# A reordered first slot in a gated scan followed by a leaky two-layer MLP

## The chip, the core and the metric

The kernel runs on one core of one Trainium2 chip. The metric is the device time of one execution in microseconds (us). All inputs and outputs are fp32 in device memory.

## What is computed

There are 4 sequences of 6080 tokens of width 256, taken as one list of 24,320 tokens. First a gated scan along each sequence, then an MLP of width 2048 on every token:

```python
sig = 1.0 / (1.0 + np.exp(-f_logit))
f = lower_bound[None, None, :] + (1.0 - lower_bound[None, None, :]) * sig
for t in range(S):
    h = f[:, t] * h + (1.0 - f[:, t]) * x[:, t]
    y[:, t] = h
...
h = y @ w_in
g = np.maximum(0.01 * h, h)
out = g @ w_out
```

## The kernel before

**Precision.** A product of two fp32 matrices is made of three matmuls in a rounded fp32 type: each operand is split into a high part (ScalarE copies it with rounding) and a low part (VectorE subtracts the high part from the operand), and low x high, high x high and high x low are added up in PSUM. For the weights, `scale_w` (L91, two ScalarE instructions), `decode_w` (L101, two of VectorE and one of GpSimd) and `split_w` (L115, one of ScalarE and one of VectorE) take the raw 64-bit words apart and split them, group by group. `wi_h` and `wi_l` are the parts of w_in, `wo` holds those of w_out, `yh` and `yl` those of the scanned y, and `gh` and `gl` those of the activation.

**Blocks, groups, slots.** The tokens go through in 24 blocks of 1024 (the last has 768), each as two halves of 512. The width of 2048 is cut into 8 groups of 256. One (block, group) pair is a slot; there are 192, numbered s. A slot's first products are a 2 x 2 scheme over (half of the group h, token half t) and its second products multiply the activations by w_out. Block 0 uses `plain_slot` (L329): four quarters of 6 matmuls, and 24 second ones, 48 in all. The later blocks use `slot` (L356): seven products M1 to M7 of 3 matmuls on combined operands, and 24 second ones, 45 in all. Of the 24 second matmuls of a slot, those of quarter (0,0) run at the slot's own end and the other 18 in the next slot (`old`).

**Order.** Every engine runs its instructions in the order in which the program writes them, so the order in the source is the schedule. A slot calls `hook(name)` at fixed places (C, a0, A, a2, B, a3, D, E), and a table (L231) and the loop at L511 hang other work there:

```python
(2, "a0"): [("th", 0)],
(2, "A"): [("f", 0), ("tx", 0), ("tx", 1)],
```

In group 2 of each block the next block's x is thus turned by two VectorE transposes (`tx`, L201), straight after the gate `f`. In block 0 the hooks also prepare the weights of the next groups: scale and decode of w_out at C, its split at a2, scale and decode of the next w_in at B, its split at E. From slot 6 to slot 13 `combine_w` (five VectorE sums) and `split_c` make the combined weights of one group per slot, at D and E in block 0, at C and a3 in block 1.

**The first slot** (`first_slot`, L444) turns the first block with TensorE against an identity matrix (`turn_first`, 4 transposes for 512 tokens of one half of the width), runs `tanh` on ScalarE, the gate's multiply-add, the product `u` and the scan on VectorE, and splits w_in group 0 whole:

```python
tanh_first(0, 0)
scale_w("i", 0)
scan_first(0, 0)
decode_w("i", 0)
```

It then does the two quarters of token half 0 (L461, L463), turns and scans token half 1, does its two quarters, and the second products of quarter (0,0) (L488). The first 512 tokens are loaded in pieces of 256 KB, the second in pieces of 512 KB, all from SP's queue (L498 to L506); `lower_bound` comes from ScalarE's queue.

**Queues and buffers.** All other loads and all stores are issued by SP. `xld`, `lld` and the output tile `osb` share two buffers in turn. PSUM has two banks for `a`, one each for `b` and `c`, and four for the second products, which the first slot also uses for turning. `a` and `r`, the two tiles of a weight being decoded, have one buffer each. `gh` and `gl` have four each.

**The end.** After the last slot (L549) the open second products run, VectorE turns the four outputs into `osb` (L288), and SP issues eight stores (L293).

Of the kernel before, what the change touches and what calls it, by code (L numbers as in the profile page):

```python
# [24 lines left out]
def tile_gated_scan_then_leaky_mlp(  # L25
# [65 lines left out]
    def scale_w(kind, g):  # L91
        a = dw_p.tile([P, 2, 256], F32, tag="a", name="a")
        r = dw_p.tile([P, 2, 256], U32, tag="r", name="r")

        hi, lo = raw_t[kind, g][:, :, :, 1], raw_t[kind, g][:, :, :, 0]
        act(out=a, in_=hi.bitcast(F32), func=ACTF.Abs, scale=2.0 ** -112)

        act(out=r, in_=lo, func=ACTF.Copy, scale=2.0 ** -29)
        part_t[kind, g] = a, r

    def decode_w(kind, g):  # L101
        hi = raw_t.pop((kind, g))[:, :, :, 1]
        a, r = part_t[kind, g]
        w = dw_p.tile([P, 4, P], F32, tag="w", name="w", bufs=2)
        au = a.bitcast(U32)
# [5 lines left out]
        wu = w.rearrange("p (h k) f -> p h (k f)", h=2).bitcast(U32)  # L111
        nc.gpsimd.tensor_tensor(out=wu, in0=au, in1=r, op=ALU.add)
        part_t[kind, g] = w

    def split_w(kind, g):  # L115
        w = part_t.pop((kind, g))
# [65 lines left out]
    def form(j, i):  # L182
# [4 lines left out]
        if i == (0, 2):  # L187
            v = b[:, :, 0]
# [6 lines left out]
    def x_piece(j, piece):  # L195
# [38 lines left out]
        (2, "A"): [("f", 0), ("tx", 0), ("tx", 1)],  # L234
# [14 lines left out]
    def product(bank, j, g, m, start, stop=True):  # L249
# [3 lines left out]
        for s, (a, b) in enumerate(((wi_l, yh), (wi_h, yh), (wi_h, yl))):  # L253
            nc.tensor.matmul(  # L254
                out=bank[:, :n], lhsT=a[:, g, w, :], rhs=b[:, i, :n],
                start=start and s == 0, stop=stop and s == 2, skip_group_check=True,
# [6 lines left out]
    def second(j, g, h, t):  # L263
# [8 lines left out]
        for k, w, v, s in ((0, 1, gh, 0), (0, 0, gh, 1), (1, 1, gh, 0), (1, 0, gh, 1), (0, 0, gl, 2), (1, 0, gl, 2)):  # L272
# [312 lines left out]
```

## Time and profile before

| | us |
|---|---|
| median of 3 runs | 2036.8 |
| lowest and highest run | 2036.34, 2039.99 |
| the profiled execution | 2041.47 |
| its span, first to last instruction | 2039.7 |

The span is what the rows below are measured in: their times count from its start. The profiled execution is 4.67 us above the median. Engines are PE (TensorE; PEld are its weight loads), DVE (VectorE), ACT (ScalarE), POOL (GpSimd) and SP. An instruction's row has its start, its duration, engine, line, operation, output<-inputs and shape, and in brackets how long its engine stood idle before it and what ended that. Where a row says x2 or more, it stands for so many like instructions and the duration is from the start of the first to the end of the last. Matmul durations overlap: the distance from one start to the next is the price, not the duration. The granted clock PEclk is a share of 2.4 GHz. A row of the windows view has the stretch, its length, the busy time of PE, PEld, DVE, ACT and POOL in it (with instructions), the granted clock, the DMA engines' mean busy share and the GB/s.

### The profile page before, as it was taken

What the parts mean: (1) busy time and instruction counts of PE and PEld (TensorE: products, weight loads), DVE (VectorE), ACT (ScalarE), POOL (GpSimd) and SP (SyncE); (2) the same over time, 40 slices, a digit from 0 to 9 for tenths busy, and PEclk for the clock granted to TensorE, in tenths of its full rate; (3) what the DMA queues carried; (4) which work ended last, traced back from release to release, by engine and by line L of the source; (5) the groups of instructions that cost most, each with busy time, mean ns of one, the idle gap of its engine ahead of it and who ended that gap; (6) DMA issues with size and microseconds to landing.
All of it is one profiled execution on the core that took longest, in us unless ns stands there. A gap on an engine that the chain in (4) does not pass through costs nothing.

```text
span 2039.7 us, 23146 instructions
## 1 busy us (share of the span) xinstructions
PE 1991.5 (98%) x8696; PEld 1625.8 (80%) x8696; DVE 1419.9 (70%) x2003; ACT 1398.6 (69%) x2344; POOL 26.8 (1%) x24
## 2 busy tenths in 40 slices
PE   5899999999999999999999999999999999999998
PEld 4777787888878788888888788888888888888888
DVE  5887666766766767667676667676766777676664
ACT  4766666677666766777667666777666766776665
POOL 1200000000000000000000000000000000000000
PEclk8999999999999999999999999999999999999999
DMA  7351505326053141560613505325054051450211
GB/s 162 91 61 18 63 1 62 40 23 63 4 59 52 11 62 16 48 62 1 63 29 34 63 1 63 43 20 63 9 54 58 5 62 23 41 57 0 37 21 16
DMA packets 583392, 84.60 MB, mean 41 GB/s; under 512 B 574064, under 2 KB 581232, under 8 KB 583280
## 3 DMA queue, kind: packets, MB, share of 16 engines
q1 hardware_dynamic: 583008, 83.13, 33.6%
q8 instruction: 68, 1.11, 0.2%
q14 instruction: 44, 0.36, 0.1%
q10 hardware_dynamic: 272, 0.00, 0.0%
HBM read 58.20 MB, written 24.90 MB: 41 GB/s over the span
## 4 chain that ended last, share of the span: by engine, by line
PE 74%; DVE 8%; DMA 7%; ACT 5%; SPq 4%; issue 2%; POOL 0%; DVEq 0%; POOLq 0%
PE o L273 39%; PE pa L254 20%; PE pc L254 10%; DMA xld<-in_x_dram 7%; PE pb L254 5%; SPq L150 4%; DVE lT L201 2%; ACT c L305 2%; ACT gh L300 2%; DVE xT L201 1%; DVE gl L310 1%; DVE c L379 1%; DVE c L397 1%; ACT c L366 0%; DVE xT L174 0%
## 5 line engine op out<-in xcount | busy, mean ns | idle before, releaser
L273 PE MATMUL o<-gh,wo 128*128 128x512 f32 (+1 forms) x3072 | 821.1, 389 | 2.6 <-DVE wo L123 2.6
L310 DVE TENSOR_TENSOR gl<-c,gh 128x512 fp32r<-128x512 f32 (+1 forms) x768 | 526.5, 689 | 275.0 <-ACT c L305 275.0
L273 PEld LDWEIGHTS o<-gh,wo 128*128 128x128 f32 x3072 | 575.8, 188 | 124.0 <-issue 3.0
L300 ACT ACTIVATE gh<-c 128x512 fp32r<-128x512 f32 (+1 forms) x552 | 342.3, 620 | 198.2 <-DVE c L397 155.8
L273 PE MATMUL o<-gl,wo 128*128 128x512 f32 (+1 forms) x1536 | 473.8, 390 | 0.0
L305 ACT ACTIVATE c<-c 128x512 f32<-128x512 f32 (+1 forms) x552 | 346.5, 628 | 17.5
L273 PEld LDWEIGHTS o<-gl,wo 128*128 128x128 f32 x1536 | 288.3, 188 | 60.5
L254 PE MATMUL pa<-yh,wi_l 128*128 128x512 f32 (+1 forms) x768 | 302.8, 394 | 15.5 <-ACT yh L225 6.9
L254 PE MATMUL pa<-yl,wi_h 128*128 128x512 f32 (+1 forms) x768 | 300.5, 391 | 0.0
L254 PE MATMUL pa<-yh,wi_h 128*128 128x512 f32 (+1 forms) x768 | 299.7, 390 | 0.0
L378 ACT ACTIVATE c<-pa 128x512 f32<-128x512 f32 (+1 forms) x184 | 109.3, 594 | 184.9 <-PE pa L254 181.9
L373 ACT ACTIVATE c<-pa 128x512 f32<-128x512 f32 (+1 forms) x184 | 109.4, 594 | 172.8 <-PE pa L254 170.4
L379 DVE TENSOR_TENSOR c<-pc,c 128x512 f32<-128x512 f32 (+1 forms) x184 | 125.2, 681 | 98.2 <-ACT c L378 94.0
L254 PEld LDWEIGHTS pa<-yh,wi_l 128*128 128x128 f32 x768 | 144.9, 189 | 58.4 <-ACT c L366 12.7
L370 DVE TENSOR_TENSOR c<-pb,c 128x512 f32<-128x512 f32 (+1 forms) x184 | 125.8, 684 | 77.9 <-PE pb L254 66.0
L397 DVE TENSOR_TENSOR c<-pc,c 128x512 f32<-128x512 f32 (+1 forms) x184 | 125.9, 684 | 64.9 <-PE pc L254 64.3
L254 PEld LDWEIGHTS pa<-yl,wi_h 128*128 128x128 f32 x768 | 144.8, 189 | 30.9 <-DVE yl L228 1.0
L254 PEld LDWEIGHTS pa<-yh,wi_h 128*128 128x128 f32 x768 | 144.8, 189 | 30.0
L254 PE MATMUL pc<-yh,wi_l 128*128 128x512 f32 (+1 forms) x384 | 152.4, 397 | 9.9 <-DVE c L379 5.9
L254 PE MATMUL pc<-yl,wi_h 128*128 128x512 f32 (+1 forms) x384 | 150.0, 391 | 0.0
L254 PE MATMUL pc<-yh,wi_h 128*128 128x512 f32 (+1 forms) x384 | 149.7, 390 | 0.0
L300 ACT ACTIVATE gh<-pa 128x512 fp32r<-128x512 f32 (+1 forms) x200 | 115.8, 579 | 14.6 <-PE pa L254 14.6
(74 smaller groups left out, 1661.9 us busy)
## 6 DMA issues: line engine op xcount, KB each, us to landing
out_dram<-osb SPq DMA_DIRECT2D x184, 128.0 KB, 3.3
lld<-in_f_logit_dram SPq DMA_DIRECT2D x90, 256.0 KB, 6.6
xld<-in_x_dram SPq DMA_DIRECT2D x90, 256.0 KB, 5.8
raw<-in_moe_w_in_dram SPq DMA_DIRECT2D x16, 256.0 KB, 3.5
raw<-in_moe_w_out_dram SPq DMA_DIRECT2D x8, 512.0 KB, 3.7
lld<-in_f_logit_dram SPq DMA_DIRECT2D x4, 192.0 KB, 5.9
xld<-in_x_dram SPq DMA_DIRECT2D x4, 192.0 KB, 4.7
out_dram<-osb SPq DMA_DIRECT2D x8, 96.0 KB, 2.5
```

The source lines that it names most:

```text
L150: nc.sync.dma_start(out=t[32 * q:32 * q + 32], in_=v[q])
L201: nc.vector.transpose(out=xs[j, nm][:, k], in_=loaded[j, nm][:, k].rearrange("p t d -> p (t d)"))
L254: nc.tensor.matmul(out=bank[:, :n], lhsT=a[:, g, w, :], rhs=b[:, i, :n], start=start and s == 0, stop=stop and s == 2, skip_group_check=True,)
L273: nc.tensor.matmul(out=o[k][:, :n], lhsT=wo[:, g, h, w, k * P:(k + 1) * P], rhs=v[:, :n], start=first and s == 0, stop=last and s == 2, sk ...
L300: act(out=gh[:, :n], in_=src[:, :n], func=ACTF.Prelu, alpha=0.01)
L305: act(out=dst[:, :n], in_=src[:, :n], func=ACTF.Prelu, alpha=0.01)
L310: vtt(out=gl[:, :n], in0=c[:, :n], in1=gh[:, :n].bitcast(F32), op=ALU.subtract)
L370: vtt(out=c11[:, :n], in0=b[:, :n], in1=c11[:, :n], op=ALU.add)
L373: act(out=c12[:, :n], in_=a[:, :n], func=ACTF.Copy)
L378: act(out=c22[:, :n], in_=a[:, :n], func=ACTF.Copy)
L379: vtt(out=c22[:, :n], in0=c[:, :n], in1=c22[:, :n], op=ALU.add)
L397: vtt(out=c12[:, :n], in0=c[:, :n], in1=c12[:, :n], op=ALU.add)
```

## The change

The first slot's work is put in another order. w_in group 0 is scaled, decoded and split in two halves (`hs`); the two quarters of token half 0 are each opened with the operand half k=0, token half 1 is turned and scanned between their parts, and their k=1 parts follow. The gate's multiply-add goes to ScalarE. Short runs of matmuls of the identity with itself (`keep_busy`, result unused) are put before and between the turns. w_in group 1 is split within the first slot, and the second products of quarter (0,0) of slot 0 move into slot 1. In the plain slots the hooks move: w_out's split and w_in's scale and decode to a new W, ahead of `low` of the first quarter; w_in's split to a new V, ahead of the last leaky pair. In block 1 `combine_w` goes to B and `split_c` to E, at the slot's end. The x transposes move from A to B and a3. For the last block's closing second products the matmuls are sorted by output, and three of its eight stores are issued by ScalarE. The first piece of x is loaded from ScalarE's queue, ahead of `lower_bound`; the second 512 tokens come in 256 KB pieces; w_in 1 is loaded ahead of w_out 0.

The body of `first_slot` after the change (after the line `j, g = 0, 0`):

```python
        h0, h1 = slice(0, 1), slice(1, 2)
        keep_busy(5)
        turn_first(0, 0)
        keep_busy(2)
        turn_first(1, 0)
        keep_busy(4)
        gate_first(0, 0)
        u_first(0, 0)
        scale_w("i", 0, h0)
        decode_w("i", 0, h0)
        scan_first(0, 0)
        scale_w("i", 0, h1)
        decode_w("i", 0, h1)
        gate_first(1, 0)
        u_first(1, 0)
        high(0)
        split_w("i", 0, "hl", h0)
        lower(0)
        split_w("i", 0, "h", h1)
        p11 = plain_bank(0, 0)
        plain_halves(p11, j, g, 0, 0, 0, (1, 0, 2))
        turn_first(0, 1)
        gate_first(0, 1)
        scan_first(1, 0)
        split_w("i", 0, "l", h1)
        p21 = plain_bank(1, 0)
        plain_halves(p21, j, g, 1, 0, 0, (1, 2, 0))
        turn_first(1, 1)
        high(1)
        lower(1)
        gate_first(1, 1)
        u_first(0, 1)
        scan_first(0, 1)
        plain_halves(p11, j, g, 0, 0, 1)
        plain_halves(p21, j, g, 1, 0, 1)
        u_first(1, 1)
        scale_w("i", 1)
        high(3)
        scan_first(1, 1)
        decode_w("i", 1)
        lower(3)
        p22, p12 = plain_bank(1, 1), plain_bank(0, 1)
        plain_halves(p22, j, g, 1, 1, 0)
        plain_halves(p12, j, g, 0, 1, 0)
        high(2)
        lower(2)
        plain_halves(p22, j, g, 1, 1, 1)
        plain_halves(p12, j, g, 0, 1, 1)
        load_w("i", 2)
        load(1, "l")
        load_w("o", 1)
        load(1, "x")
        c11 = plain_leaky(j, g, 0, 0, p11)
        scale_w("o", 0)
        decode_w("o", 0)
        low((j, g, 0, 0), c11)
        split_w("i", 1, "hl")
        c22 = plain_leaky(j, g, 1, 1, p22)
        low((j, g, 1, 1), c22)
        split_w("o", 0, "hl")
        c21 = plain_leaky(j, g, 1, 0, p21)
        low((j, g, 1, 0), c21)
        c12 = plain_leaky(j, g, 0, 1, p12)
        low((j, g, 0, 1), c12)
```

The rest of the diff, its helpers of one line left out:

```diff
+    def scale_w(kind, g, hs=slice(0, 2)):
+        if (kind, g) not in part_t:
+            a = dw_p.tile([P, 2, 256], F32, tag="a", name="a")
+            r = dw_p.tile([P, 2, 256], U32, tag="r", name="r")
+            w = dw_p.tile([P, 4, P], F32, tag="w", name="w", bufs=2)
+            part_t[kind, g] = a, r, w
+        a, r, _ = part_t[kind, g]
+
+        hi, lo = raw_t[kind, g][:, hs, :, 1], raw_t[kind, g][:, hs, :, 0]
+        act(out=a[:, hs], in_=hi.bitcast(F32), func=ACTF.Abs, scale=2.0 ** -112)
+
+        act(out=r[:, hs], in_=lo, func=ACTF.Copy, scale=2.0 ** -29)
...
+        wu = w.rearrange("p (h k) f -> p h (k f)", h=2)[:, hs].bitcast(U32)
+        nc.gpsimd.tensor_tensor(out=wu, in0=au, in1=r[:, hs], op=ALU.add)
+
+    def split_w(kind, g, part, hs=slice(0, 2)):
+        w = part_t[kind, g][2].rearrange("p (h c) f -> p h c f", h=2)[:, hs]
         if kind == "i":
-            wh, wl = wi_h[:, g, 0:4], wi_l[:, g, 0:4]
+            wh, wl = (t[:, g, 0:4].rearrange("p (h c) f -> p h c f", h=2)[:, hs] for t in (wi_h, wi_l))
         else:
-            wh, wl = (wo[:, g, :, i, :].rearrange("p h (c f) -> p h c f", c=2) for i in range(2))
-            w = w.rearrange("p (h c) f -> p h c f", h=2)
-        act(out=wh, in_=w, func=ACTF.Copy)
-        vtt(out=wl, in0=w, in1=wh.bitcast(F32), op=ALU.subtract)
+            wh, wl = (wo[:, g, hs, i, :].rearrange("p h (c f) -> p h c f", c=2) for i in range(2))
+        if "h" in part:
+            act(out=wh, in_=w, func=ACTF.Copy)
+        if "l" in part:
+            vtt(out=wl, in0=w, in1=wh.bitcast(F32), op=ALU.subtract)
...
-        (2, "A"): [("f", 0), ("tx", 0), ("tx", 1)],
+        (2, "A"): [("f", 0)],
+        (2, "B"): [("tx", 0)],
+        (2, "a3"): [("tx", 1)],
...
-        for k, w, v, s in ((0, 1, gh, 0), (0, 0, gh, 1), (1, 1, gh, 0), (1, 0, gh, 1), (0, 0, gl, 2), (1, 0, gl, 2)):
+        order = ((0, 1, gh, 0), (0, 0, gh, 1), (1, 1, gh, 0), (1, 0, gh, 1), (0, 0, gl, 2), (1, 0, gl, 2))
+        if last and j == NB - 1:
+            order = sorted(order, key=lambda v: v[0])
+        for k, w, v, s in order:
...
-            nc.sync.dma_start(out=v[q][:, :, t * nb:(t + 1) * nb], in_=osb[32 * q:32 * q + 32])
+            e = nc.scalar if j == NB - 1 and (t or q > 1) and q % 2 else nc.sync
+            e.dma_start(out=v[q][:, :, t * nb:(t + 1) * nb], in_=osb[32 * q:32 * q + 32])
...
+    def plain_halves(bank, j, g, h, t, k, order=(0, 1, 2)):
+        product(bank, j, g, (2 * h + k, ((0, 1), (3, 2))[t][k]), k == 0, k == 1, order)
+
+    def plain_leaky(j, g, h, t, bank):
         c = new_c()
         leaky_high((j, g, h, t), bank)
         leaky((j, g, h, t), c, bank)
         return c
 
+    def plain_bank(h, t):
+        pool, tag = (ps_b, "bc"[h == 0]) if t else (ps_a, "a")
+        return pool.tile([P, HM], F32, tag=tag, name="p" + tag)
...
-        c11 = plain_quad(j, g, 0, 0, a)
+        c11 = plain_leaky(j, g, 0, 0, plain_quad(j, g, 0, 0))
+        if s == 1:
+            b = plain_quad(j, g, 1, 1)
+            second(j, 0, 0, 0)
         hook("a0")
         hook("A")
+        hook("W")
         old(s, 1, 1)
         low((j, g, 0, 0), c11)
-        b = ps_b.tile([P, HM], F32, tag="b", name="pb")
-        c22 = plain_quad(j, g, 1, 1, b)
-        hook("a2")
+        if s > 1:
+            b = plain_quad(j, g, 1, 1)
+        c22 = plain_leaky(j, g, 1, 1, b)
         hook("B")
         old(s, 1, 0)
         low((j, g, 1, 1), c22)
-        a = ps_a.tile([P, HM], F32, tag="a", name="pa")
-        c21 = plain_quad(j, g, 1, 0, a)
+        c21 = plain_leaky(j, g, 1, 0, plain_quad(j, g, 1, 0))
         hook("a3")
         hook("D")
         old(s, 0, 1)
         low((j, g, 1, 0), c21)
-        c = ps_b.tile([P, HM], F32, tag="c", name="pc")
-        c12 = plain_quad(j, g, 0, 1, c)
-        hook("E")
+        b = plain_quad(j, g, 0, 1)
+        hook("V")
+        c12 = plain_leaky(j, g, 0, 1, b)
         second(j, g, 0, 0)
         low((j, g, 0, 1), c12)
+        hook("E")
...
+    def turn_first(k, t):
+        for nm in "lx":
+            if t == 0:
+                pool, tag = (ps_b, "bc"["lx".index(nm)]) if k else (ps_a, "a")
+            else:
+                pool, tag = ps_o, f"o{k}{'lx'.index(nm)}"
+            o = pool.tile([P, 4, P], F32, tag=tag, name="p" + tag)
+            for u in range(4):
+                nc.tensor.transpose(o[:, u], loaded[0, nm][:, 4 * t + u, k * P:(k + 1) * P], ident)
+            parts[nm, k, t] = o.rearrange("p u n -> p (u n)")
+
+    def keep_busy(n):
+
+        o = ps_o.tile([P, HM], F32, tag="o11", name="po11")
+        for _ in range(n):
+            nc.tensor.matmul(out=o[:, :P], lhsT=ident, rhs=ident, start=True, stop=True)
+
+    def gate_first(k, t):
+        f = xs[0, "l"][:, k, t * HM:(t + 1) * HM]
+        act(out=f, in_=parts["l", k, t], func=ACTF.Tanh, scale=0.5)
+        act(out=f, in_=f, func=ACTF.Identity, scale=cc[:, k:k + 1], bias=cd[:, k:k + 1])
...
+        load_first(nc.sync, "l", 0, 0)
+        load_first(nc.scalar, "x", 0, 0)
+        nc.scalar.dma_start(out=lb, in_=lower_bound.rearrange("(k p) -> p k", p=P))
+        load_w("i", 0)
+        for k, t in ((1, 0), (0, 1), (1, 1)):
             for nm in "lx":
-                load_first(nm, 0, slice(k, k + 1))
-            if k == 0:
-                load_w("i", 0)
-        for nm in "lx":
-            load_first(nm, 1, slice(0, KC))
+                load_first(nc.sync, nm, t, k)
+        load_w("i", 1)
...
-                    elif at == "a2":
-                        split_w("o", g)
-                    elif at == "B" and g + 1 < NG:
-                        scale_w("i", g + 1)
-                        decode_w("i", g + 1)
-                        if g + 2 < NG:
-                            load_w("i", g + 2)
-                    elif at == "E" and g + 1 < NG:
-                        split_w("i", g + 1)
+                    elif at == "W":
+                        split_w("o", g, "hl")
+                        if g + 1 < NG:
+                            scale_w("i", g + 1)
+                            decode_w("i", g + 1)
+                            if g + 2 < NG:
+                                load_w("i", g + 2)
+                    elif at == "V" and g + 1 < NG:
+                        split_w("i", g + 1, "hl")
                 if j > 0 and (g, at) == (0, "C"):
                     new_osb(j - 1)
                     if j + 1 < NB:
                         load(j + 1, "l")
                 c = s + 2 - NG
                 if 0 <= c < NG:
-                    if at == ("D" if j == 0 else "C"):
+                    if at == ("D" if j == 0 else "B"):
                         combine_w(c)
-                    elif at == ("E" if j == 0 else "a3"):
+                    elif at == "E":
                         split_c(c)
                 if j > 0:
                     for p in hooks_own.get((g, at), ()):
```

## Rows read from the trace of the kernel before

**Rows 1.** The page, part 1: busy time, share, instructions.

```profile
PE 1991.5 (98%) x8696; PEld 1625.8 (80%) x8696; DVE 1419.9 (70%) x2003; ACT 1398.6 (69%) x2344; POOL 26.8 (1%) x24
```

**Rows 2.** PE's waits, 0 to 140 us: total, times, longest.

```profile
PE pa L254 <- ACT yh L225: 6.9, 1, 6.9
PE pa L254 <- DVE wi_l L123: 6.6, 6, 1.4
PE pb L254 <- ACT yh L225: 6.5, 1, 6.5
PE o L273 <- DVE wo L123: 2.6, 1, 2.6
```

**Rows 3.** The timeline of PE at five slot starts.

```profile
52.77 0.50 PE L254 MATMUL pa<-yh,wi_l 128*128 128x512 f32 x1 [1.04 <-DVE wi_l L123]
...
125.84 0.39 PE L254 MATMUL pa<-yh,wi_l 128*128 128x512 f32 x1
...
205.82 0.39 PE L254 MATMUL pa<-yh,wi_l 128*128 128x512 f32 x1
...
216.12 0.39 PE L254 MATMUL pa<-yh,wi_l 128*128 128x512 f32 x1
...
1964.89 0.33 PE L254 MATMUL pa<-yh,wi_l 128*128 128x384 f32 x1
```

**Rows 4.** A stretch by windows, and two products of the timeline after it.

```profile
30.00:32.00 2.00, 2.00 (x5) 1.50 (x6) 1.97 (x4) 0.00 (x0) 0.16 (x1) 0.50 0.91 80
...
33.00 0.63 PE L254 MATMUL pc<-yh,wi_h 128*128 128x512 f32 x1
...
33.42 0.63 PE L254 MATMUL pc<-yl,wi_h 128*128 128x512 f32 x1
```

**Rows 5.** The timeline of the first slot, four instructions.

```profile
4.40 1.09 PE L427 MATMUL pa<-ident,lld 128*128 128x128 f32 x4 [4.40 <-DMA lld<-in_f_logit_dram]
...
5.53 0.60 ACT L431 ACTIVATE lT<-pa 128x512 f32<-128x512 f32 x1 [2.99 <-PE pa L427]
...
7.63 1.22 DVE L174 TENSOR_TENSOR_SCAN xT<-lT,xT 128x512 f32<-128x512 f32 x1
...
9.21 0.69 DVE L107 SCALAR_TENSOR_TENSOR a<-a,raw 128x512 uint32<-128x512 uint32 x1
```

**Rows 6.** The timeline: GpSimd's add, a scan beside it, the gate.

```profile
66.87 2.12 POOL L112 TENSOR_TENSOR w<-a,r 128x512 uint32<-128x512 uint32 x1 [4.06 <-DVE a L107]
...
67.87 2.21 DVE L174 TENSOR_TENSOR_SCAN xT<-lT,cy,xT 128x512 f32<-128x512 f32 x1
...
68.84 1.25 ACT L207 ACTIVATE lT<-lT,cd,cc 128x1024 f32<-128x1024 f32 x1
```

**Rows 7.** Windows: the fullest plain slot.

```profile
102.03:114.74 12.71, 11.28 (x49) 8.94 (x49) 10.92 (x20) 9.46 (x18) 3.18 (x2) 1.00 0.76 62
```

**Rows 8.** The timeline of a slot that turns x, and M6 behind.

```profile
320.75 0.39 PE L254 MATMUL pa<-yh,wi_l 128*128 128x512 f32 x1
...
326.90 0.63 ACT L305 ACTIVATE c<-c 128x512 f32<-128x512 f32 x1
...
327.17 2.37 DVE L201 STREAM_TRANSPOSE xT<-xld 128x1024 f32<-128x1024 f32 x2 [3.41 <-DMA xld<-in_x_dram]
...
332.09 0.68 DVE L397 TENSOR_TENSOR c<-pc,c 128x512 f32<-128x512 f32 x1
...
334.64 0.19 PEld L254 LDWEIGHTS pa<-yh,wi_l 128*128 128x128 f32 x1 [0.48 <-ACT c L366]
```

**Rows 9.** The end: SP's issues, their landing, two windows (of loads first).

```profile
2031.47 5.50 SPq L293 DMA_DIRECT2D out_dram<-osb  x8
...
out_dram<-osb SPq DMA_DIRECT2D x8, 96.0 KB, 2.5
...
28.00:30.00 2.00, 0.15 (x1) 0.16 (x1) 1.46 (x4) 1.15 (x2) 0.00 (x0) 0.50 1.60 145
2034.00:2035.00 1.00, 0.00 (x0) 0.00 (x0) 0.00 (x0) 0.00 (x0) 0.00 (x0) 0.73 0.92 138
```

More of the change, by code (lines that the diff above doesn't have):

```diff
@@ L89, in load_w, with decode_w @@
         raw_t[kind, g] = r
[L91 to L105, printed above, removed]
+    def scale_w(kind, g, hs=slice(0, 2)):
[8 more added lines that the diff above has]
+        act(out=r[:, hs], in_=lo, func=ACTF.Copy, scale=2.0 ** -29)
+    def decode_w(kind, g, hs=slice(0, 2)):
+        hi = raw_t[kind, g][:, hs, :, 1]
+        a, r, w = part_t[kind, g]
+        au = a[:, hs].bitcast(U32)
         nc.vector.tensor_scalar(out=hi, in0=hi, scalar1=0x80000000, scalar2=None, op0=ALU.bitwise_and)
@@ L246, in tile_gated_scan_then_leaky_mlp, with product @@
     hooks_own = {(0, "C"): [("l", (5, 7))]}
-    def product(bank, j, g, m, start, stop=True):
+    def product(bank, j, g, m, start, stop=True, order=(0, 1, 2)):
         yh, yl = ysplit[j]
@@ L252, in product @@
         w, i = m
-        for s, (a, b) in enumerate(((wi_l, yh), (wi_h, yh), (wi_h, yl))):
+        for e, s in enumerate(order):
+            a, b = ((wi_l, yh), (wi_h, yh), (wi_h, yl))[s]
             nc.tensor.matmul(
                 out=bank[:, :n], lhsT=a[:, g, w, :], rhs=b[:, i, :n],
-                start=start and s == 0, stop=stop and s == 2, skip_group_check=True,
+                start=start and e == 0, stop=stop and e == 2, skip_group_check=True,
             )
@@ L418, in load_first, with u_first @@
         )
[L420 to L433 removed]
+    def turn_first(k, t):
[16 more added lines that the diff above has]
+        act(out=f, in_=f, func=ACTF.Identity, scale=cc[:, k:k + 1], bias=cd[:, k:k + 1])
+    def u_first(k, t):
         r = slice(t * HM, (t + 1) * HM)
         f, u = xs[0, "l"][:, k, r], xs[0, "x"][:, k, r]
[L436 to L438 removed]
         nc.vector.scalar_tensor_tensor(
@@ L441, in scan_first, with high, lower @@
         )
-        scan(0, k, r.start, r.stop)
+    def scan_first(k, t):
+        scan(0, k, t * HM, (t + 1) * HM)
+    def high(i):
+        x_piece(0, ("h", (i, i + 1)))
+    def lower(i):
+        x_piece(0, ("l", (i, i + 1)))
     def first_slot():
         j, g = 0, 0
-        for nm, k in (("l", 0), ("x", 0), ("l", 1), ("x", 1)):
-            turn_first(nm, k, 0)
-        tanh_first(0, 0)
-        scale_w("i", 0)
-        scan_first(0, 0)
-        decode_w("i", 0)
-        tanh_first(1, 0)
@@ L454, in first_slot @@
-        split_w("i", 0)
-        scan_first(1, 0)
-        new_split(0)
-        x_piece(0, ("h", (0, 2)))
-        x_piece(0, ("l", (0, 2)))
-        scale_w("o", 0)
-        a = ps_a.tile([P, HM], F32, tag="a", name="pa")
-        c11 = plain_quad(j, g, 0, 0, a)
-        a = ps_a.tile([P, HM], F32, tag="a", name="pa")
-        c21 = plain_quad(j, g, 1, 0, a)
-        for nm, k in (("l", 0), ("x", 0), ("l", 1), ("x", 1)):
-            turn_first(nm, k, 1)
-        tanh_first(0, 1)
-        tanh_first(1, 1)
@@ L477, in first_slot @@
         load(1, "x")
-        scale_w("i", 1)
+        c11 = plain_leaky(j, g, 0, 0, p11)
+        scale_w("o", 0)
+        decode_w("o", 0)
         low((j, g, 0, 0), c11)
-        low((j, g, 1, 0), c21)
-        b = ps_b.tile([P, HM], F32, tag="b", name="pb")
-        c22 = plain_quad(j, g, 1, 1, b)
-        decode_w("i", 1)
-        split_w("o", 0)
-        c = ps_b.tile([P, HM], F32, tag="c", name="pc")
-        c12 = plain_quad(j, g, 0, 1, c)
-        low((j, g, 1, 1), c22)
-        second(j, g, 0, 0)
-        split_w("i", 1)
+        split_w("i", 1, "hl")
+        c22 = plain_leaky(j, g, 1, 1, p22)
+        low((j, g, 1, 1), c22)
+        split_w("o", 0, "hl")
+        c21 = plain_leaky(j, g, 1, 0, p21)
+        low((j, g, 1, 0), c21)
+        c12 = plain_leaky(j, g, 0, 1, p12)
         low((j, g, 0, 1), c12)
     with tc.manual_schedule():
-        nc.scalar.dma_start(out=lb, in_=lower_bound.rearrange("(k p) -> p k", p=P))
         make_identity(nc, ident)
```

48 lines of the change are left out of this document (13 added, 35 removed).

## The prediction

> **What bounds the kernel now.** I read the page's busy times first: TensorE is busy for 1991.5 us of the span, so only stretches in which it waits or runs at its lower clock can give time back [rows 1]. To find those I read its waits: in the first 140 us it waits 6.9 us and 6.5 us for a rounded half of y, 2.6 us for the first w_out group, and six times, 6.6 us in all, for `wi_l` at the start of a slot [rows 2]. Then the slot starts. From block 2 on a slot is 45 matmuls (21 first products, 24 second): 10.30 us from 205.82 to 216.12, 0.229 us each [rows 3]. The six plain slots from 52.77 to 125.84 hold 6 x 48 matmuls, 65.9 us by that price, and take 73.1: 7.2 lost. The seven slots from 125.84 to 205.82 take 80.0 for 72.1: 7.9 lost. The 169 slots from 205.82 to 1964.89 take 1759.1 for 1740.7: 18.4 lost, 0.87 in each of 21 blocks. Ahead of 52.77 stand 24 + 6 + 48 matmuls, 17.9 us of work, so 34.9 us went into loading, turning, scanning and waiting. That is the bigger purse, and the change aims at it.
>
> The clock belongs to it: from 30 to 32 us the granted clock is 0.50, the 1.2 GHz level, and products start 0.42 us apart (33.00 and 33.42) where later ones start 0.229 apart, at 2.4 GHz; the idle 6.5 us stand just ahead of that stretch [rows 2, 4].
>
> **The first slot.** Its new order is a chain through VectorE. Start: `tanh` ran at 5.53 for 0.60 [rows 5]. x's first piece now goes out beside f's on ScalarE's queue; sharing may hold f's up by 0 to 0.8 us, I take 0.3. The multiply-add moves from VectorE to ScalarE: 1.25 us for 1024 [rows 6], so about 0.7 for 512. The first `u` starts at 5.53 + 0.3 + 0.6 + 0.7 = 7.1. From there to `wi_l` of group 1, which lets slot 1 begin, VectorE has in program order:
> - ten instructions 512 wide (four `u`, four `lower`, one `low`, one `wi_l`), 0.65 from start to start where one lasts 0.69: 6.5;
> - four scans of 1.22 and two carry copies: 5.1 [rows 5];
> - two whole decodes, the shift of 0.69 and its mask, estimated at 0.4: 2.2 [rows 5];
> - for the w_in halves two half decodes and two half subtractions, between half and whole of those; nearest half: 2.0.
>
> That is 15.8. GpSimd's four adds (two half, two whole) lie beside it, and a scan beside one took 2.21 instead of 1.22 [rows 5, 6]: 1.0 for a whole, 0.5 for a half, 3.0 (bounds 0 and 4). VectorE then waits once, for yh of k=1: ScalarE's copy is queued behind the gate of the second half, and that behind TensorE's turning, which stands behind the first three products: 1.4 (0 to 2.2). Another 0.4 goes where `w_out` 0's scale waits for GpSimd to release its tile. Sum 7.1 + 15.8 + 3.0 + 1.4 + 0.4 = 27.7. The 24 products of slot 0 end before that if the clock is up (the last six follow `lower(2)` at about 24.3), and at about 27.9 if it is down.
>
> Slot 1 now holds 54 matmuls, since the second products of slot 0's first quarter moved into it: 12.4, so 40.1. Its end waits about 0.8 for group 2's split, because the two f transposes stand ahead of that decode on VectorE. Slot 2 starts at 40.9 instead of 52.77: **11.9 gained**, bounds 9.5 and 13.5.
>
> What costs nothing here: the eleven `keep_busy` matmuls have no row; a product at the low clock (0.42) is my value for one, the turns' 0.27 (4 in 1.09) the lower end [rows 4, 5]. Five end near 3.6, ahead of the first load; two lie ahead of the second load; four end near 10.9, ahead of the first product near 11.2. With that cover gone they add up to 1. SP's queue keeps its loads; the second halves go out as four DMAs of half the size, w_in 1 goes ahead of w_out 0, and both are wanted after 19 us. `lower_bound` moves behind x on ScalarE's queue, some 0.5 later, hidden by the turning and `tanh`; if not, the first `u` is late by that. Whether TensorE is at 2.4 GHz when slot 1 starts is unseen: products run nearly unbroken up to it, so I take yes; if no, some ten matmuls (as many as the trace shows slow in a stretch) cost 0.2 more each, 2 us.
>
> **The plain slots.** The next group's split moves ahead of the last leaky pair, so `wi_l` should be ready when the slot ends. What is late next is VectorE: busy 10.92 of the 12.71 us of the fullest slot [rows 7], against 10.98 for 48 matmuls. It fits, barely. I walk a slot: `low` at 0, decode, GpSimd at 1.8 to 3.4, split, second decode, GpSimd from 6.9 to 8.5, split copy to 9.2, `wi_l` by 9.9: 1.1 to spare. With the combine and the four differences in slot 6 the spare is gone, and I charge 1.0 there. Of 7.2 lost **6.2 return**, bounds 3.5 and 7.2.
>
> **Block 1.** The combine moves behind the first `low`, its split to the slot's end. The combine is one 512-wide sum and four 128-wide ones, some 1.6 us (an estimate from the 0.69 of a 512-wide instruction [rows 5]). The slot's last sum is no longer held by the split's wait, but the split's two ScalarE copies, some 0.6, now stand ahead of the next slot's c11 copy, which M6 waits for: by the walk of the next part M6 comes about 0.65 late in five slots, 1.1 more in the one that also evacuates block 0, and 2.9 where combine and transposes meet. That is 7.3 lost for 7.9: **0.6 gained**, bounds -2 and 3.
>
> **x turned later.** In each block the two x transposes stand ahead of the c22 sum and waited 3.41 us for their DMA in the block shown; they last 1.18 each [rows 8]. The first `low` starts when ScalarE's leaky copy ends, 6.8 us into the slot (327.53 after 320.75), and ends at 7.45. Moved behind it and ahead of the c12 sum, the transposes no longer wait: this DMA landed 6.4 into the slot. The new wait: the first transpose ends at 8.6, the next `low` at 9.25, the second transpose at 10.4, so the c12 sum ends at 11.1, 0.8 us into the next slot. Queued behind it on ScalarE are both leaky copies, then the next slot's c11 copy, and M6 waits for that. In the block shown the sum ended at 332.77 and the wait of M6's weight load ended at 334.64, 1.87 later [rows 8]. So M6 starts 0.8 + 1.87 = 2.67 into the slot instead of 2.06, and with its restart the block loses about 0.73 instead of 0.87: 21 x 0.14 = **3.0 gained** in this execution, bounds -5 (0.24 worse a block) and 8.
>
> **The end.** With the last block's second products sorted by output, the first output is complete three matmuls sooner: the first stores go out 0.35 earlier. Three of eight stores move to ScalarE's queue. The trace speaks both ways: the eight issues fill 5.50 us on SP, and each lands a constant 2.5 us after its issue, so nothing piles up in the engines and issue is the limit; but meanwhile the DMA share is 0.92 at 138 GB/s, and 128-byte packets of loads did no more than 145 GB/s at a share of 1.60 [rows 9]. I take engines near their limit: 0.35 + 0.4 = **0.8**, bounds 0.35 and 2.5. The Trainium skill's page "DMA: Bandwidth & Descriptors", section "Issuing engines are not separate DMA queues", holds that DMAs from several engines run on the same 16 engines and only the sequencer's issue time is saved. By that rule, with the engines taken as full, the term would be 0.35, and the sum 0.4 less; the share of 0.92 leans its way, the constant landing time does not.
>
> **Sum.** 11.9 + 6.2 + 0.6 + 3.0 + 0.8 = 22.5. The profiled execution took 2041.47 us, 4.7 over the median of 2036.8, so the sum gives 2019.0 from it. If that 4.7 is the recorder's, the runs come to 2014.3; if it is x landing late, which the new order no longer waits for, they come to 2019. I say 2017.
>
> **Rivals.**
> - **VectorE becomes the bound** of block 0: GpSimd's adds cost 4 and the wait for yh 2.2, so slot 2 starts 1.8 later, and six plain slots run 0.8 over, so of the 7.2 only 2.4 return, 3.8 less; block 1, as full, gives nothing. In all 6.2 less: 2023. For it: 10.92 busy of 10.98 wanted [rows 7]; against: that count holds the contention already. 0.16.
> - **All terms at their better ends**: the clock up from the first product, stores limited by issue, the x transposes free: 1.6, 1.0, 1.7 and 5 better than my terms, 2008. The constant landing time speaks for it. 0.13.
> - **Slower**: the c12 sum. It decides the M6 of the next slot in 22 blocks; each further us of lateness is a us lost. The other terms bring 19.5, so from 0.87 + 0.93 = 1.8 lost a block on the kernel is slower. It would be paid if the second transpose slid behind a late ScalarE pair by 1.5 us: 2.2 a block, 21 x 1.35 = 28 lost against 19.5, so 9 slower than now, 2046. For it: ScalarE is in order there; against: my walk leaves its `low` waiting 0.0. 0.04.
> - **The order is changed but not the time**: the loads set the first slot whatever follows, and what the plain slots gain is lost to VectorE: within 4 us of 2036.8. Against: TensorE's first waits name y, not loads [rows 2]. 0.04.
>
> My forecast has 0.63. It and the better rival lie below 2032.7, as does the VectorE rival: faster by over 0.2% (4 us, about what a measurement here can tell from no change) 0.92, within 0.04, slower 0.04. The forecast's own range is 2011 to 2022, from 2 at the start, 5 at the transposes and the 4.7 taken together; reaching to the two rivals beside it, 2008 to 2026.
>
> **What would show it.** In the new trace: slot 2's first product near 41; no wait for `wi_l` at slot starts above 0.3, except after slot 6; no VectorE wait for x in the later blocks, and M6 waits of about 0.6 after the transposes' slot; the last store's issue end 0.4 to 2.5 us nearer to the last transpose. I am wrong if slot 2 starts after 44, if plain slots last over 11.8, or if blocks lose over 1.2 each.

## The result and the profile after the change

| | us |
|---|---|
| median after, 4 runs (2017.07 to 2018.91) | 2017.28 |
| median before, 4 runs on the same chip (2036.34 to 2041.52) | 2038.39 |
| ratio, with its 95% interval | 0.9897 (0.988 to 0.9914) |
| the profiled execution after, and its span | 2017.16, 2015.3 |

The change is faster by 1.0%. The prediction was 2017.0. The two spans differ by 24.4 us (2039.7 and 2015.3), and the sum had 22.5. A span is given to 0.1 us, and so is what is worked out from one below. First the page's busy times, to be held against [rows 1]:

```profile
PE 1988.0 (99%) x8718; PEld 1627.1 (81%) x8718; DVE 1417.0 (70%) x2003; ACT 1399.3 (69%) x2352; POOL 28.0 (1%) x25
```

TensorE does the same work, with 22 short instructions more, and is busy for 3.5 us less. The rest of the 24.4 us, 20.9, is time in which it stood idle. Its waits in the first 140 us, as in [rows 2] (total, times, longest):

```profile
PE pa L259 <- DVE wi_l L125: 3.8, 4, 1.4
PE pb L259 <- DVE yl L230: 2.6, 1, 2.6
PE pb L259 <- ACT yh L227: 1.4, 1, 1.4
```

The two long waits for a rounded half of y (6.9 and 6.5) and the wait for the first w_out group are gone; in place of the first two stand 2.6 and 1.4. Of the waits for `wi_l` four are left, one in the first slot and three at slot starts. The slot starts of the changed kernel, in TensorE's timeline, against [rows 3]:

```profile
28.06 0.50 PE L259 MATMUL pa<-yh,wi_l 128*128 128x512 f32 x1 [1.43 <-DVE wi_l L125]
...
40.54 0.39 PE L259 MATMUL pa<-yh,wi_l 128*128 128x512 f32 x1
...
52.45 0.50 PE L259 MATMUL pa<-yh,wi_l 128*128 128x512 f32 x1 [0.76 <-DVE wi_l L125]
...
97.64 0.51 PE L259 MATMUL pa<-yh,wi_l 128*128 128x512 f32 x1 [0.96 <-DVE wi_l L125]
...
108.76 0.39 PE L259 MATMUL pa<-yh,wi_l 128*128 128x512 f32 x1
...
187.40 0.39 PE L259 MATMUL pa<-yh,wi_l 128*128 128x512 f32 x1
...
1940.15 0.34 PE L259 MATMUL pa<-yh,wi_l 128*128 128x384 f32 x1
```

These are the starts of slots 1, 2, 3, 7, 8, 15 and of the last block. From them and [rows 3] each term of the sum can be read off:

| stretch | before | after | gained | predicted |
|---|---|---|---|---|
| up to slot 2 | 52.77 | 40.54 | 12.2 | 11.9 |
| slots 2 to 7 | 73.07 | 68.22 | 4.85 | 6.2 |
| slots 8 to 14 | 79.98 | 78.64 | 1.3 | 0.6 |
| 169 slots, 15 to 183 | 1759.07 | 1752.75 | 6.3 | 3.0 |
| last block to the end of the span | 74.81 | 75.15 | -0.34 | 0.8 |
| sum | | | 24.4 | 22.5 |

Four terms have the sign forecast. The end has not: it became longer. The issues in the timeline, against [rows 9]:

```profile
2006.44 5.62 SPq L302 DMA_DIRECT2D out_dram<-osb  x5
2006.44 2.54 ACTq L302 DMA_DIRECT2D out_dram<-osb  x3
```

The same stores in the view of DMA issues, with the median time from issue to landing in the last column:

```profile
out_dram<-osb SPq DMA_DIRECT2D x5, 96.0 KB, 4.2
out_dram<-osb ACTq DMA_DIRECT2D x3, 96.0 KB, 4.1
```

And windows among them and at their end:

```profile
2009.00:2010.00 1.00, 0.00 (x0) 0.00 (x0) 0.00 (x0) 0.00 (x0) 0.00 (x0) 0.50 1.02 146
...
2012.00:2013.00 1.00, 0.00 (x0) 0.00 (x0) 0.00 (x0) 0.00 (x0) 0.00 (x0) 0.50 0.75 113
2013.00:2014.00 1.00, 0.00 (x0) 0.00 (x0) 0.00 (x0) 0.00 (x0) 0.00 (x0) 0.50 0.55 82
```

SP needs 5.62 us for five issues where it needed 5.50 for eight, and a store lands 4.2 us after its issue where it took 2.5. From the first issue to the end of the span it is 8.9 us (2015.3 less 2006.44), before it was 8.2. SP's last issue ended at 2012.06, and from there on the DMA engines were no longer full.

### The profile page after: what moved, and what is told of

Same layout as the page of the kernel before. It is cut to its first block, busy times and chain, and to the rows that moved or that the text cites. A ratio compares the mean times of both kernels' runs of the same rounds, so it can differ in the third digit from the quotient of the medians.

```text
span 2015.3 us, 23212 instructions
## 1 busy us (share of the span) xinstructions
PE 1988.0 (99%) x8718; PEld 1627.1 (81%) x8718; DVE 1417.0 (70%) x2003; ACT 1399.3 (69%) x2352; POOL 28.0 (1%) x25
## 4 chain that ended last, share of the span: by engine, by line
PE 90%; DVE 6%; ACT 3%; issue 1%; DMA 0%; POOL 0%; DVEq 0%; POOLq 0%; ACTq 0%
PE o L281 48%; PE pa L259 25%; PE pc L259 11%; PE pb L259 6%; DVE xT L203 3%; DVE gl L319 1%; ACT c L314 1%; ACT gh L309 1%; DVE c L420 1%; ACT c L389 1%; DMA lld<-in_f_logit_dram 0%; DVE xT L176 0%; ACT wi_h L140 0%; DVE wi_l L125 0%; DVE osb L296 0%
```

## The experiments

Each kernel is the changed one with the edit shown. The first eight times are of one run each, beside a run of the kernel before at 2039.29 us; the last four are medians. A slot is priced at 10.30 us, so the 169 slots cost 1740.7 and what they take beyond that is lost.

**All last stores from SP.** The sorted products stay.

```diff
-            e = nc.scalar if j == NB - 1 and (t or q > 1) and q % 2 else nc.sync
-            e.dma_start(...)
+            nc.sync.dma_start(...)
```

> The changed kernel with all last stores from SP, the sorted last products kept. The change's tail, from the last product's end to the end of the span, is 8.46 us, before it was 8.12. Theory, the DMA engines are full and the second queue only mixes the stores: 8 issues of 0.66 again, begun 0.3 earlier than in the kernel before, so a tail of about 7.8, 0.6 shorter than the changed kernel's. Rival, issue is the limit and two queues help, the loss lies elsewhere: the tail grows to 9 or more.

Measured: 2018.46 us, span 2016.7. The start of the last block and the issues in its timeline:

```profile
1942.14 0.34 PE L259 MATMUL pa<-yh,wi_l 128*128 128x384 f32 x1
...
2008.43 5.49 SPq L301 DMA_DIRECT2D out_dram<-osb  x8
```

Their landing in the view of DMA issues, and after it windows:

```profile
out_dram<-osb SPq DMA_DIRECT2D x8, 96.0 KB, 2.5
```

```profile
2011.00:2012.00 1.00, 0.00 (x0) 0.00 (x0) 0.00 (x0) 0.00 (x0) 0.00 (x0) 0.92 0.95 141
...
2014.00:2015.00 1.00, 0.00 (x0) 0.00 (x0) 0.00 (x0) 0.00 (x0) 0.00 (x0) 0.50 0.97 146
```

From the last block on it takes 74.6 us, 0.6 less than the change and 0.2 to 0.3 less than before. So the sorting brings 0.2 to 0.3 of its 0.35, and the second queue costs 0.6. Single executions settle this, since it repeats: all eight profiled kernels with the second queue take 75.1 to 75.2 from there on, all five with one queue 74.5 to 74.7. Eight stores of 96 KB in 5.49 us are 143 GB/s, what the windows show the DMA engines moving, and with two queues the eight issues took 5.62 us in all: they were paced by the draining, and the issue time was no limit of its own. With one queue the engines are near full up to 2015, less than 2 us before the end; with two they run down sooner. Why the mix drains worse no run tells. This run is still 1.3 us above the profiled one of the change, because TensorE's clock was down when slot 1 began and slot 8 started 2.0 later; that is taken up below.

**x turned at A again, and the second transpose at the slot's end.** Two kernels:

```diff
-        (2, "A"): [("f", 0)],
-        (2, "B"): [("tx", 0)],
-        (2, "a3"): [("tx", 1)],
+        (2, "A"): [("f", 0), ("tx", 0), ("tx", 1)],
```

> The changed kernel with both x transposes back ahead of the c22 sum (A). Theory, they wait there for their DMA and that made 18.4 us lost in the 169 slots before the last block where the changed kernel loses 12.5: the loss returns to 17 to 20, VectorE waits for x in most blocks, and the losses differ from block to block (0.6 to 1.8). Rival, the 6 us come from another part: the loss stays at 12 to 13.

```diff
-        (2, "a3"): [("tx", 1)],
+        (2, "E"): [("tx", 1)],
```

> The changed kernel with the second x transpose moved on to the slot's end (E), behind the c12 sum. Theory, the c12 sum's lateness (0.67 us into the next slot, M6 1.87 later) is all of the 0.60 us that each block still loses: the M6 wait goes, the 169 slots lose under 2 us instead of 12.5, and the span falls by 10 to 12. Rival, the transpose only hands the lateness on to the next slot's c11 sum (1.5 us late there) and through it to a later wait: 0.3 or more lost a block, span lower by at most 6.

Measured: 2021.3 us with both at A. The 169 slots take 1755.7 there and lose 15.0, between the two expectations. VectorE stands before the transposes again, and the sum behind them holds up TensorE inside the same slot, here in the timeline of one block:

```profile
308.88 2.37 DVE L203 STREAM_TRANSPOSE xT<-xld 128x1024 f32<-128x1024 f32 x2 [3.05 <-DMA xld<-in_x_dram]
...
311.89 0.50 PE L257 MATMUL pc<-yh,wi_l 128*128 128x512 f32 x1 [0.66 <-DVE c L400]
```

So later turning is worth 3.0 of the 6.3 us gained in this stretch. Ahead of this stretch it costs 0.2 in slots 2 to 7 and 0.9 in slots 8 to 14, which take 67.99 and 77.78 here. The other 3.3 lies between this kernel and the one before, whose order in these slots is the same: VectorE's waits for x add up to 47.3 us here and 53.4 before. What a block loses differs from one to the next in both, from 0 to 1.8. Whether x landed sooner by chance or by the new start is not shown.

Measured: 2003.07 us with the second transpose at E, span 2001.3, 14.0 less than the change. Slots 8, 15 and the last block start here:

```profile
107.97 0.39 PE L259 MATMUL pa<-yh,wi_l 128*128 128x512 f32 x1
...
185.49 0.39 PE L259 MATMUL pa<-yh,wi_l 128*128 128x512 f32 x1
...
1926.19 0.34 PE L259 MATMUL pa<-yh,wi_l 128*128 128x384 f32 x1
```

The 169 slots take 1740.70: nothing is lost any more. The span fell by more than the 10 to 12 expected, since slots 2 to 7 (0.5) and 8 to 14 (1.1) gained too. For the reason compare the slot that turns x, in the changed kernel's timeline first:

```profile
227.46 1.23 DVE L203 STREAM_TRANSPOSE xT<-xld 128x1024 f32<-128x1024 f32 x1
...
228.62 0.65 DVE L420 TENSOR_TENSOR c<-pc,c 128x512 f32<-128x512 f32 x1
...
230.51 0.58 ACT L389 ACTIVATE c<-pa 128x512 f32<-128x512 f32 x1
...
231.14 0.51 PE L259 MATMUL pa<-yh,wi_l 128*128 128x512 f32 x1 [0.15 <-ACT c L389]
```

and then in that of the kernel with the transpose at E:

```profile
225.56 0.68 DVE L420 TENSOR_TENSOR c<-pc,c 128x512 f32<-128x512 f32 x1
...
226.69 0.39 PE L259 MATMUL pa<-yh,wi_l 128*128 128x512 f32 x1
...
228.21 1.24 DVE L203 STREAM_TRANSPOSE xT<-xld 128x1024 f32<-128x1024 f32 x1
...
228.75 0.39 PE L259 MATMUL pa<-yh,wi_l 128*128 128x512 f32 x1
```

In the change the c12 sum runs behind the second transpose and ends 0.67 us into the slot that starts at 228.60. With the transpose behind it, the sum ends 0.45 us ahead of the slot start at 226.69, and M6 comes 2.06 into the slot, on time.

**The weights' preparation where it was.** w_out's split back at a2, w_in's scale and decode at B, its split behind the last leaky pair:

```diff
-                    elif at == "W":
+                    elif at == "a2":
                         split_w("o", g, "hl")
-                        if g + 1 < NG:
-                            ...
+                    elif at == "B" and g + 1 < NG:
+                        ...
...
+        c12 = plain_leaky(j, g, 0, 1, b)
         hook("V")
-        c12 = plain_leaky(j, g, 0, 1, b)
```

> The changed kernel with the weights' preparation of the plain slots back in its old places (w_out's split behind the second leaky pair, w_in's scale and decode at B, w_in's split behind the last leaky pair). Theory, that place is what made each slot start wait for wi_l: waits of about 1.0 us return at the six starts from slot 2 on, and the stretch from the start of slot 2 to that of slot 8 is 72 to 73.5 us instead of 68.2. Rival, VectorE fills these slots anyway: 68 to 69.5.

Measured: 2023.63 us. TensorE's waits from 0 to 190 us show it:

```profile
PE pa L259 <- DVE wi_l L125: 9.1, 8, 1.4
```

Six of the eight stand at the ends of slots 1 to 6, 1.04 to 1.43 each, and slots 2 to 7 take 73.4 us, as before the change (73.07). So the moved hooks are the whole gain there, and the rival fell. In the change two of these waits are left. The 0.76 at the end of slot 2 is missing in both kernels that turn x elsewhere: in the change the transposes at B and a3 stand ahead of w_in's split. (With one at E, 0.27 comes a slot later.)

**The second products of slot 0's first quarter in slot 0 again.**

```diff
             b = plain_quad(j, g, 1, 1)
-            second(j, 0, 0, 0)
...
         c12 = plain_leaky(j, g, 0, 1, p12)
+        second(j, g, 0, 0)
```

> The changed kernel with the second products of slot 0's first quarter back in slot 0, ahead of slot 1's products. Theory, they hold TensorE until w_out group 0 is split (29.2 us in the changed kernel), so slot 1 starts at 30.6 to 31 instead of 28.1 and slot 2 at 41.3 to 42 instead of 40.5, beside 2 us more if the clock is down. Rival, slot 2 is set by VectorE's weights: it starts within 0.3 of the changed kernel's 40.5 or of its late 42.5.

Measured: 2020.34 us. TensorE waits for w_out's split, in its timeline, and the window behind it has the low clock:

```profile
29.37 2.08 PE L281 MATMUL o<-gh,wo 128*128 128x512 f32 x4 [2.67 <-DVE wo L125]
...
32.09 0.60 PE L259 MATMUL pa<-yh,wi_l 128*128 128x512 f32 x1
```

```profile
30.00:32.00 2.00, 2.00 (x6) 1.61 (x5) 1.77 (x4) 1.29 (x3) 0.00 (x0) 0.50 1.67 142
```

Slot 1 starts at 32.09, 1 us later than expected, and slot 2 at 43.32, 2.8 later than in the change: the order holds TensorE up, and the clock fell behind that wait. The rival fell.

**Without the keep_busy matmuls.** The three calls are left out.

> The changed kernel without the eleven unused matmuls of the identity. Theory, VectorE's chain sets slot 1's start: the products of the first slot run at the 1.2 GHz level up to about 18 us and slot 1 starts at 28.1 to 28.8 (28.06 with them). Rival, the clock they hold is worth a stretch of ten slow products: slot 1 starts at 30 or later.

Measured: 2019.3 us. The first products are slow, and slot 1 starts at 28.78, also slow:

```profile
11.41 0.79 PE L259 MATMUL pa<-yh,wi_h 128*128 128x512 f32 x1 [1.46 <-ACT wi_h L123]
...
28.78 0.80 PE L259 MATMUL pa<-yh,wi_l 128*128 128x512 f32 x1 [1.61 <-DVE wi_l L125]
```

This run could not settle more: three of the kernels that keep these matmuls also had the low clock at slot 1 (one queue, x at A, and the split at A below).

**The combine of block 1 where it was, and its split in the next slot.**

```diff
-                    if at == ("D" if j == 0 else "B"):
+                    if at == ("D" if j == 0 else "C"):
...
-                    elif at == "E":
+                    elif at == ("E" if j == 0 else "a3"):
```

> The changed kernel with block 1's combine and its split back at C and a3. The seven slots from slot 8 on lose 6.5 us in the changed kernel, 7.9 before. Theory, the two places trade one wait for another: 6 to 8 lost, now as waits for the c12 sum, 0.5 to 1.1 each, instead of 0.6 for the c11 copy. Rival, the new place is worth several us by itself: 10 or more lost.

```diff
-                    elif at == "E":
+                    elif at == "E" and j == 0:
                         split_c(c)
+                if at == "A" and 0 < c <= NG and j > 0 and ("c", c - 1) in part_t:
+                    split_c(c - 1)
```

> The changed kernel with block 1's split of the combined weights moved on to A of the next slot, behind the c11 and c12 copies. Theory, the 0.6 us that M6 waits in these slots come from the split's two ScalarE copies ahead of the c11 copy: the waits of 0.33 and 0.77 go, the seven slots lose 2 to 3.5 us instead of 6.5. Rival, the lateness is VectorE's (the combine ahead of the c12 sum): at least 5 lost still.

Measured: 2017.6 and 2019.57 us. Slots 8 to 14 lose 7.0 in the first and 6.7 in the second, against 6.5 in the change. The waits only change their name. In the first they are five for the c12 sum; in the second the c11 copy's waits fall to 0.17 at most and the c12 sum's come up, as their lines from 0 to 190 us say, the first kernel's ahead:

```profile
PE pc L259 <- DVE c L420: 3.0, 5, 0.8
```

```profile
PE pc L259 <- DVE c L420: 2.3, 3, 1.7
PE pa L259 <- ACT c L389: 0.9, 6, 0.2
```

The theory for the second kernel fell: with the split's two ScalarE copies out of the way of the c11 copy the time does not come back. The rival's number held, at least 5 lost. Its reason, that VectorE is late in block 1 wherever the split stands, fits the waits for the c12 sum; but the edit moves the split's two VectorE subtractions as well, so the two engines' shares are not separated.

**Both improvements together, and the clock.** Four kernels have one queue and the second transpose at E. One is that alone, one has no keep_busy, one has the first of these edits beside it, one has both:

```diff
-        plain_halves(p22, j, g, 1, 1, 0)
+        product(p22, j, g, (2, 3), True, False, (0, 1))
+        keep_busy(8)
+        product(p22, j, g, (2, 3), False, False, (2,))
...
         plain_halves(p12, j, g, 0, 1, 1)
+        keep_busy(8)
```

> The changed kernel with two edits together: every last store from SP (sorted products kept), and the second x transpose at the slot's end, E. If the two gains are independent: 2003.07 of the run with the transpose at E, less the 0.59 us by which the last block and tail were shorter with one queue, so 2002.5 with the clock up at slot 1; 2.0 more (2004.5) in runs in which it is still down then, so runs spread over 2 us. Rival: the two shortened the same wait at the end of the last block, then 2003.1. Ratio to the kernel before about 0.982.

> The same without any keep_busy matmul, in 5 rounds. Theory, after the first look without them: they hold the clock up only for the first products (which then start slow, 0.4 us apart), not for slot 1, whose clock is decided by the 2.63 us wait for yl near 20 us; then the median is 0 to 0.8 us above the kernel with them, and its runs spread over the same 2 us. Rival: they do decide the clock at slot 1; then every run is 2 us above the fastest run of the kernel with them, with no spread.

> The same as the first with keep_busy, plus 8 more such matmuls put into the wait for yl (between the second and third product of quarter (1,1), k=0), some 2.0 us of TensorE work at 2.4 GHz in an idle stretch of 2.6. Theory: the wait is what drops the clock, so the granted clock stays 1.00 from 20 to 34 us, slot 1 starts at or before 28.1 and slot 2 at 40.5 at most in every run, and the runs agree within 0.5 us at or 0.2 to 0.6 below the fastest run without the filler (the products from 22.9 on no longer run slow). Rival: the clock falls for another reason (it falls anyway between 20 and 26 us), then the runs spread as without it. If the filler delays yl's products, slot 1 starts later than 28.5 with the clock at 1.00.

> The kernel with one filler (8 keep_busy matmuls in the wait for yl) and 8 more behind slot 0's last first product, ahead of slot 1. With the first filler alone the granted clock stayed 1.00 until 28 us, the products ended at 25.6 instead of 27.0, and TensorE then waited 2.48 us for wi_l and the clock fell at 29 to 33. Theory: what drops the clock is an idle stretch of some 2.5 us wherever it stands, and VectorE's chain makes one of that length in all ahead of slot 1; with both parts filled (1.95 us each) the clock stays 1.00 from 20 to 34, slot 1 starts at 27.8 to 28.3, slot 2 at 40.3 to 40.7, slot 8 at 107.9 to 108.3, and every run is 2002.4 to 2003.1, about the fastest runs without fillers. Rival: the clock falls again somewhere between 26 and 36 us though no idle stretch above 1 us is left; then slot 8 starts 1 to 2 us later and the runs lie at 2003.3 to 2004.6 as with one filler.

The kernel before ran at 2039.49 us beside the first three and at 2040.38 beside the last.

| kernel | median (lowest to highest) us | ratio to before, 95% |
|---|---|---|
| both improvements | 2002.88 (2002.67 to 2004.51) | 0.9823 (0.981 to 0.9837) |
| and no keep_busy | 2003.65 (2003.61 to 2004.84) | 0.9827 (0.9813 to 0.984) |
| and one filler | 2004.42 (2003.26 to 2004.57) | 0.9828 (0.9815 to 0.9841) |
| and two fillers | 2002.99 (2002.74 to 2003.07) | 0.9817 (0.9804 to 0.9831) |

The two improvements add up: from the last block's start to the end it is 74.5 us, as with one queue alone, and 2002.7 in the best runs is 0.4 below the transpose at E alone. The highest run, 2004.51, is the profiled one. Windows of it:

```profile
20.00:22.00 2.00, 0.00 (x0) 0.00 (x0) 1.93 (x5) 1.52 (x3) 0.09 (x1) 0.90 1.61 147
22.00:24.00 2.00, 1.60 (x4) 1.31 (x5) 2.00 (x2) 0.58 (x2) 1.48 (x1) 0.50 1.42 151
...
28.00:30.00 2.00, 2.00 (x5) 1.61 (x6) 1.72 (x4) 2.00 (x5) 0.00 (x0) 0.50 1.63 130
```

TensorE waited 2.63 us for yl here, the granted clock fell to 0.50, the 1.2 GHz level, and it stayed there beyond the start of slot 1 at 27.81. Slot 2 then started at 42.15. In the change the same wait brought it down for a shorter time:

```profile
22.00:24.00 2.00, 1.33 (x3) 1.14 (x4) 2.00 (x3) 0.57 (x2) 1.56 (x1) 0.57 1.65 127
24.00:26.00 2.00, 2.00 (x7) 1.53 (x6) 1.70 (x4) 1.60 (x4) 0.10 (x1) 0.58 1.20 216
26.00:28.00 2.00, 0.63 (x3) 0.19 (x1) 2.00 (x3) 1.57 (x3) 1.45 (x1) 1.00 1.34 216
```

That is a difference of some 2 us between executions that have the same order, and by its size most of the spread of the runs. Without keep_busy slot 1 started at 28.98 with the clock up, and the median is 0.77 higher, at the upper end of what the theory gave. So these matmuls do not decide the clock at slot 1. What they give is early: fast first products, and slot 1 0.7 us (the changed kernel) to 1.2 us (this one) sooner.

With one filler the clock stayed up through that wait, and fell behind the next one. Its timeline, and then a window:

```profile
19.92 1.95 PE L458 MATMUL po<-ident 128*128 128x128 f32 x16
...
28.08 0.50 PE L259 MATMUL pa<-yh,wi_l 128*128 128x512 f32 x1 [2.48 <-DVE wi_l L125]
```

```profile
30.00:32.00 2.00, 2.00 (x7) 1.52 (x5) 1.85 (x4) 1.24 (x3) 0.00 (x0) 0.50 1.20 168
```

TensorE's products ended sooner, and it waited 2.48 us for `wi_l` in place of 0.77, since VectorE's chain sets when slot 1 can begin. Three of its four runs lie near 2004.5, and the theory that the yl wait alone drops the clock fell. With both stretches filled the granted clock is 1.00 in every window from 18 to 36 us and the five runs lie within 0.33 us. It is not faster than the best runs without fillers, as expected; it only does away with the spread. That an idle stretch of some 2.5 us is what drops the clock is not shown by this: without keep_busy it fell behind waits of 1.05 and 1.84.

## Why the prediction held, and where it did not

The time itself came closer than the reasons. The sum gave 2019.0 from the profiled execution and 2014.3 from the median, and 2017 was chosen between them; that 2017.28 was measured is partly luck.

**The first slot** was right in its chain: slot 1 at 28.06 for 27.7. The start came 0.47 late: the first `u` ran at 7.57, not 7.1. The first turn began 0.47 later than before, at 4.87 [rows 5], where 0.3 was reckoned; the gate's multiply-add took 0.81, not 0.7; the rest is gaps between instructions. The rest of the chain through VectorE took 20.5 us for the 20.6 reckoned, with the two waits in it 1.58 and 0.20 for 1.4 and 0.4. That slot 2 began at 40.54 for 40.9 is luck: slot 1 ran its 54 matmuls in 12.48, and the 0.8 that was charged at its end, behind the f transposes, did not come. The price of GpSimd's adds, 1.0 for a whole one, which I took from a single scan [rows 6], can be seen here, in the timeline of the changed kernel:

```profile
25.90 1.56 POOL L114 TENSOR_TENSOR w<-a,r 128x512 uint32<-128x512 uint32 x1 [2.16 <-DVE a L109]
...
26.24 1.76 DVE L125 TENSOR_TENSOR wi_l<-w,wi_h 128x512 fp32r<-128x512 f32 x1
```

The subtraction lasts 1.07 us more than its 0.69. It ends 0.54 after the add, at 28.00, as if it had all but stood still until 27.46. The Trainium skill's page "SBUF — State Buffer", section "SBUF: two separate sides", says that VectorE with two SBUF inputs and GpSimd exclude each other for a whole instruction, and the trace agrees. It was also the last instruction ahead of slot 1. In the kernel with two fillers the add began behind the subtraction, which then took 0.69:

```profile
27.08 1.61 POOL L114 TENSOR_TENSOR w<-a,r 128x512 uint32<-128x512 uint32 x1 [3.32 <-DVE wi_l L125]
```

```profile
26.25 0.69 DVE L125 TENSOR_TENSOR wi_l<-w,wi_h 128x512 fp32r<-128x512 f32 x1
```

Slot 1 started at 27.10 there. The profile says that the add waited for the subtraction. That fits the buffers: `w` and the identity share two, and the second filler still reads the identity, so the add has to take the one that the subtraction reads. The earlier start was gone again by slot 2, at 40.59 behind a wait of 0.56 for `wi_l`.

What I had not priced is the clock ahead of slot 1. "Products run nearly unbroken up to it" was wrong: TensorE waited 2.63 us for yl and 1.43 for `wi_l`. The 2 us named for a low clock was the right size, and by the runs it is paid in some executions and not in others.

**The plain slots** were mis-sized, 4.85 for 6.2. The 1.0 charged to slot 6 was there (0.96 at 97.64). Slots 2 and 6 last 11.91 and 12.11, over the 11.8 named as a sign of being wrong; the other four take 10.99 to 11.11. The walk left out slot 2, in which the moved x transposes stand ahead of w_in's split and cost 0.76: a collision of two parts of the same change.

**Block 1** had the right sizes: 2.9 us were reckoned where combine and transposes meet, and that slot loses 2.88; 0.65 in the others, and they lose 0.61. What was too high was the share for evacuating block 0: one slot loses 1.22 where 1.75 was reckoned. So 6.5 is lost for the 7.3 forecast. M6 does wait for the c11 copy, as walked, here in TensorE's waits from 0 to 190 us:

```profile
PE pa L259 <- ACT c L389: 2.9, 6, 0.8
```

But the split's two copies, which the walk made the reason, are not the whole price: with them moved away 6.7 is lost.

**x turned later** went as walked: the c12 sum ends 0.67 into the slot for 0.8, and M6 starts 1.87 after it, to the hundredth. Twenty blocks lose 0.60 for 0.73 and the last one 0.05, so 12.05 is lost for 15.3, and the term was 6.3 and not 3.0. Against x at A in the changed kernel it is 3.0 after all: the 18.4 that it was reckoned from did not come back there (15.0). It had a better answer in the same walk: if the sum must not stand behind a transpose, the transpose can stand behind the sum. One line brings 14 us.

**The end** is the step that failed. "I take engines near their limit: 0.35 + 0.4" gave the second queue 0.4 us; it took 0.6. (The 0.35 is two matmuls, not three: the first output is complete with the third of the six instead of the fifth.) The constant landing time of 2.5 us was read as a sign that nothing piles up, but the issues themselves were held to the rate of the drain, and so it could not show. The page "DMA: Bandwidth & Descriptors" of the Trainium skill, which would have the second queue bring nothing beyond issue time, was nearer, but the loss goes beyond it. The sum came out near, 24.4 for 22.5, because the transposes' gain stands against the plain slots' shortfall and the end's loss.

## What to carry to other kernels

Where stores leave one after another at an even spacing, divide their size by the spacing before you call the issue the limit: if that is the rate at which the DMA engines move, a second queue has nothing to give and can delay what ends last. When an engine's order is the schedule, walk what stands ahead of the instruction that releases the next stage, and put anything with slack behind it. A filled wait moves the wait, so look for the next idle stretch on the same chain before counting on the clock.

## What the runs showed of the hardware that was not expected

- With two queues a store of 96 KB landed 4.1 to 4.2 us after its issue (median), with one 2.5, and the DMA engines moved no more (146 GB/s at a share of 1.02, 146 at 0.97 with one).
- The granted clock can come back within 4 us of a 2.63 us wait, or stay down for 10, in kernels with the same order around it. It fell behind an idle stretch of 2.48 us as well, and in the kernel without keep_busy behind shorter ones, 1.05 and 1.84 us: the products, 0.23 apart from 23.7 on, are 0.43 apart from 25.7 on.
- Before its first change the granted clock is recorded as 1.00 even where products last 0.8 us and start 0.6 apart, as from 12.41 to 13.01 us without keep_busy. At the start of a profile the spacing of the products is the better witness.
